# Chunk-selected attention into an ELU MLP on one core: w_in loaded in two pieces of eight chunks, both issued ahead of a fill

## The chip, the cores and the metric

The kernel runs on one core of a Trainium2 chip. The metric is the device time of one execution in microseconds (us). Each kernel was run several times; the median of the runs stands for it. One further execution was taken by the hardware profiler, and all views of the trace come from that one.

## The reference

The inputs are q, k and v of 4 batches, 8 heads, 768 positions and 64 dimensions, and two weight matrices, w_in (512 x 2048) and w_out (2048 x 512), all float32. For each head the keys are cut into chunks of 32. Each query gets an upper bound of its score with every chunk from the chunk's smallest and largest key in each dimension, takes the six best causal chunks, and attends to those alone:

```
ub     = sum(max(q * k_min, q * k_max), axis=-1)        # causal chunks only
sel    = the six chunks with the largest ub
attn   = softmax(where(sel & causal, q k^T / sqrt(64), -1e9)) @ v
x      = attn with the heads side by side               # 3072 tokens x 512
h      = x @ w_in
out    = where(h > 0, h, exp(min(h, 0)) - 1) @ w_out
```

## The kernel before

**Units of work.** The 3072 tokens are worked on in eight units of 384 (i = 0 to 7). Units 0 and 1 take the first half of batches 0 and 1 together, 192 positions of each at a time; the other six take one half of one batch each. For each unit the kernel loads k, q and v, transposes k and q on PE (operations kT and qT; L402 for the paired units, L543 for the others), computes the bounds (ub, L592) and the chosen chunks on DVE, the scores, their exponentials on ACT, and the product with v. Unit 0 covers only the first six chunks, so it needs no choice. The attention output is transposed into four tiles xt of 128 x 384.

**The MLP of a unit** (`mlp`, L844). For each of 16 column chunks fc of w_in, four matmuls on PE (h{i}.{fc}, L851) multiply a 128 x 128 block of w_in with the xt tiles into one PSUM bank; ACT takes the exponential (e, L858), POOL or DVE subtracts one (m, L860), and DVE combines them to the activated chunk (g, L864), which frees the bank. Then w_out is multiplied in (o{i}.{tt}.{c}, L875), and the result is copied out and stored.

**The weights.** w_in and w_out stay in SBUF in bfloat16. They are float32 in HBM, and the DMAs that load them are issued by POOL, which casts on the way. w_in comes in three pieces of columns: `load_w_in(0, 0, 4)`, `load_w_in(1, 4, 8)` and `load_w_in(2, 8, 16)` (L290 and L934). An operation h{i}.{fc} waits for the one piece with its chunk. w_out comes in four pieces (L296). All other loads, k, q, v (L304) and the copies of a constant into the score operand (econst, L304), are issued by SP, but for two at the start from ACT. They read rows of 64 float32.

**What sets the order.** The program is not scheduled by a tool. Each operation is added to a graph (`g.op`), with what it reads and writes; the string ORDER then lists all operations as triples of an engine letter (P, A, D, G for POOL, S for SP) and two digits in base 64 for the number of the operation in the graph (L944). Each engine takes its own operations in that order, one after the other, and waits where an operand isn't ready. PLACES gives the buffer slot of each new buffer in the order of its first use: slots of 11 load buffers f, 8 PSUM banks and so on.

**The stretch of the change.** In the order of the program, POOL's operations from v0p1 on are:

- v0p1: cast of a v load into the tile vext (L333), for the positions of unit 0
- rz: fill of the mask rows of rhs0 with zeros (L247), read from unit 2 on
- w_in1: DMA of chunks 4 to 7
- v0p0 and v1p0: two more casts of v
- w_in0: DMA of chunks 0 to 3
- ka10p0, a copy of keys, and ks1p1, a subtraction for the bounds
- w_in2: DMA of chunks 8 to 15
- tris2 (a triangular mask), more copies and fills, then the four DMAs of w_out among the MLP's m operations

PE's operations around the first MLP are, in its order: the products with v of unit 0, kT0s0, more products and the transposes into xt, kT0s1, h0.4, h0.6, h0.5, qT0s0, h0.3, qT0s1, h0.2, h0.1, h0.7, ub00, h0.0, h0.15, h0.9, h0.14, h0.12, h0.10, h0.8, a score matmul, h0.11, another, h0.13, and from there scores of unit 1 between the products with w_out. kT0s0 and kT0s1 read the two k loads of unit 1, batch 0; qT0s0 and qT0s1 read its two q loads. SP issues these four loads right behind the v loads of unit 0, and after them the k and q loads of unit 1, batch 1, and two copies of econst.

The f buffers of the casts v0p0 and v1p0 are handed to later loads by PLACES.

Of the kernel before, what the change touches and what calls it, by code (L numbers as in the profile page):

```python
# [42 lines left out]
P1DP26P25P1ED10G0-S2PS2vS2OD27D28D1FA1wP1YP20P2aGmDA0SP29D2bP1XA2cP1+D21G0JP1IP1OP1RP1SP1HS2IP2o  # L43
P1ND1GD1JD1ZD1KP2dG1dGmFA1-P1LD2qD1PA1QD2jD22P23D1TD1UD2eA2sD24A1MS2QP1VD1WG08G2uG0hP2BD2DD2CA2t
Pm-Pn6G2EAn7GbsGmGPn2Gn8D2pG2rAm+Dn0D14D0GAn3Dn4P2wPmWA2xA2yS2RP2JA2KDn5D2zPmSPmODn9Dn1AmXAmTD2L
GmYPnaGmHDmZAmPP3lAnbGmIA2FDmQDmUPmKAmLDmVD3nD3mA2MD3pGncPnGG2HPniA2AG07GmMA1fPnCG2SAnjD3oPnuD3q
D3rPnmDmRDmNG3tPneAnHA3sGnkDndAnvGnIP3HDnlAnDPnqGnwA3IDnJP41PnyDnxAnrA3uGnEDnFP3JP3+AnfPnQDnsS2k
A3KDntD2NAnnS3fG3LP2XA42P38PnRS2mA40GmJAnzA2GDnoD2ZDnpD2YP4lGngPnKPnXA4mD3vDnhA2+A30D43D3cP4DA4E
P4FG3ePnYA4GGnAD3aA3dD39D2-D31P4jD4HP3gG3bP33PnSS32S4+A34D35PnLA3hA4kD3iG3kS2TDnBP3wD4nS2VG2lG36
D3xG3jS50PnZPn-A2nD3yD3zA37S4-D3APnMPnTD3BD3CS4YD3GA3EG3FP3NDnUP4OP4MS4XS4ZP3MD3DP48P45A4PA4NP44  # L50
G2UG2WP4aD3ODn+D3PP4IP4JA4bP3SPnNA49D46D47A3TD4cS7UP3QD4QAnOP4sP4uP4dA3RP4eP4oS7SA4tP4pD4fP5rG3U
D4gA4vP4RD4KD4LP4SP4hA5sP5QS7WD4TD4UP3VP3WA5RD4qP5fP4VD3XD3YA5gS7RP5ED4rG4wP4xA4WP4yD5SP3ZA5FD4z
# [12 lines left out]
AppGpqDprDd1ApxGpyDpzAbrD8NPpUApVDpWPpYPqgApZGqeD8PA88Gp-Dp+Pq4Pq0Pq8PqkPqlPqwPqxD8QSc+Gd0AblAaK
Aq5Aq1Aq9DpXGq2Dq3Dq6Dq7DqfA8RP8VP9aPqmGqaDqbAd4AqhGqiDqjSbqSaLGaMA8WP9bA8IA9cD9dP97A98P8XA8YPqy
P8ZA8-P93A94P95A96P8+A90PqzP91A92D8TD8UDaXD8SP9kP9oPamP9yD8xGaZA9lA9zSaFPbzP9wAbADqAPqnA9xAanD99
P9fP9eP9sP9uP9BP9mSfrScTGd7ScVSfnSd3ScWDqoA9pA9vP9CA9DGhKD9AD9gD9hA9nA9tP9XA9YPqqD9EPa-P9iD9jP9q
A9rP9PPbEA9QP9FPaoAapP9RPa0P9GPa1A9SP9ZPqrP9VGaqAa2A9-Db7GbCDbFDb6SbnSpcSb8D9HD9IDbHDa+PagP9LP9T
ParP9NA9WA9UDb0D9+PqsPacPaePasDa3A9OPa5A9MPa4Dg2Dd8Db9DbaAahAafAatAadPaiPakAalAajPaaAabPdpPbuAbv  # L70
PbJGauPawPavP9JDa6Da7Pa8PqtGfoAbGAbKA9KAhIAb1Aa9DbcDbbDaxDayAfsAquDbBDbdDbeDbLPazDaAPdaGbfDdbGde
GddShDSd6DhESfpDbyDb2DfqSftPqGAqHGqIPqKPbgShxAqLDqMAbhAbwPraArbAbiAbjGrcAbIDqJDqNSbtSd9SfhSqvDrd
DfuGbNPreArfAbkAhQGrgDrhPrmArnPqWAqXAbxPriPbODbPGqYDqZDbQArjAhJPrqAdcGroDrpDbRGrkDrlGg8DbSPr2PqO
PqCGbMArrAbDGrsDrtAr3Gr4AqPGqQAdqAqDPqSAqTGqUAg1DbTDr5DbUDqRPdfAdgPryArzPdkAdlPq-Aq+GqEDqFDfvDqV
GbVGrAPr6PruAbXAr7DbYGr0Dr1DfxPrCPb+AdhArvAbWPbZAb-Ac0PrIGr8Dr9DrBPcdPrJPcbPc2PchAceAg5GrwGdiGc1
DrxDfwDdrAccPc3Ac4PcvPcgAciPcuPcFAcwGcjPcIPcJPcrAcsPrKPcpPcDPrLDc5DcfPc6Pc7AcKDcLSqBSfjShySfyDfz
# [904 lines left out]
```

## Time and profile before

| | |
|---|---|
| median of 3 runs | 281.04 us (280.64 to 281.32) |
| profiled execution | 281.25 us |
| its span, first to last instruction | 279.5 us |
| mean granted TensorE clock | 0.999 |
| DVE, ACT, POOL busy | 78%, 78%, 45% |
| DMA moved | 38.47 MB, mean 138 GB/s |
| queue q1 (issued by SP) | 98864 packets, 33.53 MB |
| queue q0 (issued by POOL: w_in, w_out) | 3696 packets, 4.19 MB |

A row of a timeline has its start, its length, the engine, the source line, the operation with the tiles it writes and reads, how many instructions of the kind were merged, and in brackets the idle time of the engine before it with what ended it. A row of the chain of waits has start, length and what ran. A row of a DMA issue has the tiles, the issuing queue, the number of DMAs, the size and the time from issue to landing. A row of a queue has its packets, its megabytes and the time that its packets took as a share of 16 DMA engines; where it is taken for a window, it counts that window alone. In the windows' rows each engine has its busy time and, in parentheses, its instructions; behind them stand the clock, the DMA share and GB/s.

### The profile page before, as it was taken

To read this page: it belongs to the slowest core of one execution; us is meant where nothing else is said; L and a number is where in the kernel's file an instruction comes from. 1 tells how busy PE (TensorE), PEld (TensorE's weight loads), DVE (VectorE), ACT (ScalarE), POOL (GpSimd) and SP (SyncE) were. 2 spreads that over 40 slices of the span, in tenths; PEclk is the share of its full clock that TensorE was granted. 3 is DMA by queue.
4 is the path that set the end of the run, shared out by engine and by line. 5 is a ranking of instruction groups with operands and counts; after the bars stand their busy time and mean duration, and the time that the engine had idled before them with its cause. 6 is when DMAs were issued, how large, how long until landed. Compare 5 with 4: busy or idle time off the path is not lost.

```text
span 279.5 us, 6918 instructions
## 1 busy us (share of the span) xinstructions
PE 263.2 (94%) x2436; PEld 162.9 (58%) x2436; DVE 217.4 (78%) x656; ACT 217.1 (78%) x493; POOL 125.5 (45%) x249
## 2 busy tenths in 40 slices
PE   1978899999999999999999999999999999999994
PEld 0745465785456755576555555666655556665553
DVE  4668978799978999979998999569797698424931
ACT  2596796789699998999999859886968579982620
POOL 8674745348521755422685736222541346310410
PEclk9999999999999999999999999999999999999999
DMA  8999999999529999946985499416600210042002
GB/s 163 198 211 211 199 211 210 217 202 251 123 60 203 247 219 230 196 115 112 171 203 114 109 226 206 84 36 136 170 4 0 60 39 1 16 139 82 15 17 96
DMA packets 103779, 38.47 MB, mean 138 GB/s; under 512 B 95168, under 2 KB 99520, under 8 KB 103744
## 3 DMA queue, kind: packets, MB, share of 16 engines
q1 hardware_dynamic: 98864, 33.53, 57.3%
q0 software_dynamic: 3696, 4.19, 8.7%
q10 hardware_dynamic: 1184, 0.30, 0.5%
q8 instruction: 19, 0.31, 0.5%
q14 instruction: 16, 0.13, 0.1%
HBM read 30.41 MB, written 6.29 MB: 131 GB/s over the span
## 4 chain that ended last, share of the span: by engine, by line
PE 70%; DVE 13%; DMA 8%; ACT 4%; issue 1%; POOL 1%; SPq 0%; DVEq 0%; ACTq 0%
PE bank L875 24%; PE bank L851 22%; PE bank L782 9%; DMA w_in_sb<-in_moe_w_in_dram 5%; PE bank L833 5%; DVE gT L864 2%; PE bank L592 2%; PE bank L402 2%; DMA kc<-in_k_dram 2%; ACT e L858 2%; DMA f<-in_k_dram 1%; PE bank L543 1%; PE bank L728 1%; PE bank L893 1%; DVE on L646 1%
## 5 line engine op out<-in xcount | busy, mean ns | idle before, releaser
L851 PE MATMUL bank<-xt,w_in_sb 128*128 128x384 bf16 x512 | 89.2, 326 | 2.2 <-DMA w_in_sb<-in_moe_w_in_dram 2.2
L875 PE MATMUL bank<-w_out_sb,gT 128*128 128x512 bf16 x368 | 89.5, 379 | 0.0
L860 POOL TENSOR_SCALAR m<-e 128x384 f32<-128x384 f32 x96 | 50.7, 536 | 59.3 <-ACT e L858 47.0
L864 DVE SCALAR_TENSOR_TENSOR gT<-bank,m 128x384 bf16<-128x384 f32 x128 | 65.9, 549 | 9.7 <-POOL m L860 8.4
L858 ACT ACTIVATE e<-bank 128x384 f32<-128x384 f32 x128 | 58.6, 493 | 16.7 <-PE bank L851 13.9
L851 PEld LDWEIGHTS <-w_in_sb 128*128 128x128 bf16 x512 | 49.1, 98 | 36.6 <-DMA w_in_sb<-in_moe_w_in_dram 3.0
L797 ACT ACTIVATE pt<-bank 128x384 bf16<-128x384 f32 (+1 forms) x144 | 67.0, 547 | 3.5 <-PE bank L782 2.1
L875 PEld LDWEIGHTS <-gT 128*128 128x128 bf16 x368 | 34.6, 97 | 35.7 <-issue 2.2
L782 PE MATMUL bank<-rhs,lhs 96*128 96x384 bf16 (+2 forms) x240 | 42.8, 293 | 1.0 <-DVE on L646 0.5
L814 POOL TENSOR_TENSOR pt<-pt,tri 128x256 bf16<-128x256 bf16 (+1 forms) x18 | 16.6, 924 | 39.3 <-ACT pt L801 20.1
L782 PEld LDWEIGHTS <-lhs 96*128 96x128 bf16 x240 | 21.7, 97 | 13.9 <-issue 0.9
L833 PEld LDWEIGHTS <-pt 128*128 128x128 bf16 x576 | 21.0, 97 | 4.0 <-DVE pt L814 0.4
L833 PE MATMUL bank<-vext,pt 128*128 128x65 bf16 x576 | 22.2, 193 | 0.3 <-DVE pt L814 0.3
L646 DVE TENSOR_TENSOR on<-bank,rcp 128x384 bf16<-128x384 f32 (+1 forms) x37 | 18.8, 509 | 1.2
L367 DVE TENSOR_REDUCE kst<-bank 128x12 f32<-128x384 f32 x32 | 16.6, 548 | 3.7 <-PE bank L402 2.8
L322 POOL CAST rhs<-qt 64x384 bf16<-64x384 f32 x23 | 12.3, 542 | 13.1 <-ACT qt L320 12.1
L636 DVE RECIPROCAL rcp<-bank 128x6 f32<-128x6 f32 (+1 forms) x40 | 7.3, 185 | 14.0 <-PE bank L833 8.7
L320 ACT ACTIVATE o<-bank 128x512 f32<-128x512 f32 (+1 forms) x13 | 7.5, 587 | 13.0 <-PE bank L875 10.1
L322 DVE COPY o<-bank 128x512 f32<-128x512 f32 (+1 forms) x12 | 7.9, 663 | 12.0 <-PE bank L875 10.0
L860 DVE TENSOR_SCALAR m<-e 128x384 f32<-128x384 f32 x32 | 13.1, 417 | 2.8 <-ACT e L858 2.6
L402 PE MATMUL bank<-ident_f,f 96*128 96x96 f32 x64 | 9.3, 295 | 6.2 <-DMA f<-in_k_dram 6.2
L814 DVE TENSOR_TENSOR pt<-pt,tri 128x512 bf16<-128x512 bf16 (+1 forms) x30 | 10.8, 376 | 5.3 <-ACT pt L801 3.5
(102 smaller groups left out, 338.6 us busy)
## 6 DMA issues: line engine op xcount, KB each, us to landing
f<-in_v_dram SPq DMA_DIRECT2D x22, 256.0 KB, 4.8
out_dram<-o SPq DMA_DIRECT2D x21, 256.0 KB, 3.4
f<-in_q_dram SPq DMA_DIRECT2D x18, 256.0 KB, 4.9
f<-in_k_dram SPq DMA_DIRECT2D x18, 256.0 KB, 4.7
kc<-in_k_dram SPq DMA_DIRECT2D x8, 384.0 KB, 4.3
w_out_sb<-in_moe_w_out_dram POOLq DMA_DIRECT2D x4, 512.0 KB, 10.5
f<-in_q_dram SPq DMA_DIRECT2D x6, 192.0 KB, 5.0
w_in_sb<-in_moe_w_in_dram POOLq DMA_DIRECT2D x2, 512.0 KB, 8.8
```

Source lines behind the costliest of these rows:

```text
L322: eng[e].tensor_copy(out=dst, in_=src)
L367: g.op(("kmin", "kmax")[w] + tag, (DVE,), lambda e, w=w, op=op: nc.vector.tensor_reduce(out=cs(w), in_=src(), axis=AX.X, op=op), reads=[(b ...
L646: nc.vector.tensor_tensor(out=ap(on)[:, 0:nt].rearrange("p q h d -> p h q d"), in0=view()[:, :, :, 0:D], in1=ap(rcp)[:, :, 0:nt].to_broadc ...
L782: nc.tensor.matmul(ap(banks[hd])[:, o + pc:o + pc + wd], lhsT=apl(ls, G)[0:96, pr, hd, P * kb:P * (kb + 1)], rhs=ap(rs)[0:96, hd, c0 - HS ...
L797: lambda e, hd=hd, pt=pt, banks=banks, wtot=wtot: nc.scalar.activation(out=ap(pt)[:, hd, PAD:PAD + wtot], in_=ap(banks[hd])[:, 0:wtot], fu ...
L814: eng[e].tensor_tensor(out=view, in0=view, in1=tri[:, 64:64 + P].rearrange("p (a b w) -> p a b w", a=1, b=1) .to_broadcast([P, 2, len(dg), ...
L833: nc.tensor.matmul(view()[:, hd, qi, :], lhsT=ap(pt)[:, hd, P * qi + off:P * qi + off + P], rhs=ap(vx[b])[:, kb, 2 * r + hd, :], start=(kb ...
L851: nc.tensor.matmul(ap(bank)[:, 0:HS], lhsT=w_in_sb[:, kk, P * fc:P * (fc + 1)], rhs=ap(xT[i, kk]), start=(kk == 0), stop=(kk == NKK - 1))
L858: g.op(f"e{i}.{fc}", (ACT,), lambda e, eb=eb, bank=bank: nc.scalar.activation(out=ap(eb), in_=ap(bank)[:, 0:HS], func=AF.Exp), reads=[(ban ...
L860: g.op(f"m{i}.{fc}", (POOL, DVE), lambda e, eb=eb, mb=mb: eng[e].tensor_scalar(out=ap(mb), in0=ap(eb), scalar1=-1.0, scalar2=1.0, op0=AOT. ...
L864: nc.vector.scalar_tensor_tensor(out=ap(gt), in0=ap(bank)[:, 0:HS], scalar=0.0, in1=ap(mb), op0=AOT.max, op1=AOT.min),
L875: nc.tensor.matmul(ap(bank), lhsT=ap(gts[fc])[:, P * tt:P * (tt + 1)], rhs=w_out_sb[:, fc, :], start=(fc == 0), stop=(fc == NFC - 1))
```

## The change

w_in is loaded in two pieces of eight chunks, 0 to 7 and 8 to 15. In POOL's order both stand ahead of the fill rz, with the casts v0p0 and v1p0 between them:

```
v0p1, w_in0 (0-7), v0p0, v1p0, w_in1 (8-15), rz, ka10p0, ks1p1, tris2, ...
```

The orders of PE, ACT, DVE and SP, operation by operation, are the same. Since there is one operation fewer in the graph, the numbers behind it in ORDER fall by one, and many rows of the string change in text alone. The casts v0p0 and v1p0 stand earlier in the program, so the load buffers f pass on in another rotation in PLACES; no other class of buffer changes. The core of the diff (of ORDER the one row that holds most of the stretch):

```diff
-S0+D0UP1qP1uD1cP18A1nD13S2gS2fG0CA1rP1hD19A1sG0nP1zD12S2hS2iP1yA1iP1AA1gA1mGmED0PA1CP1vA1xA1BG0A
+S0+D0UP1qP1uD1cP18A1nD13S2gS2fG0CGmDG0AG0-GmEG0nA1rP1hD19A1sP1zD12S2hS2iP1yA1iP1AA1gA1mD0PA1CP1v
...
-    for i, (c0, c1) in enumerate(((0, 4), (4, 8), (8, 16))):
+    for i, (c0, c1) in enumerate(((0, 8), (8, 16))):
         load_w_in(i, c0, c1)
```

In the row, G0C is v0p1, G0n is rz, G0A and G0- are v0p0 and v1p0, and GmD, GmE (and GmF further on, before the change) are w_in0, w_in1 (and w_in2).

More of the change, by code (lines that the diff above doesn't have):

```diff
@@ L47 @@
[L47 to L52, printed above, removed]
@@ new lines @@
+A1xA1BP1DP26P25P1ED10S2PS2vS2OD27D28D1FA1wP1YP20P2aA0SP29D2bP1XA2cP1+D21G0JP1IP1OP1RP1SP1HS2IP2o
+P1ND1GD1JD1ZD1KP2dG1dA1-P1LD2qD1PA1QD2jD22P23D1TD1UD2eA2sD24A1MS2QP1VD1WG08G2uG0hP2BD2DD2CA2tPmZ
+Pn5G2EAn6GbsGmFPn1Gn7D2pG2rAm-Dm+D14D0GAn2Dn3P2wPmVA2xA2yS2RP2JA2KDn4D2zPmRPmNDn8Dn0AmWAmSD2LGmX
+Pn9GmGDmYAmOP3lAnaGmHA2FDmPDmTPmJAmKDmUD3nD3mA2MD3pGnbPnFG2HPnhA2AG07GmLA1fPnBG2SAniD3oPntD3qD3r
+PnlDmQDmMG3tPndAnGA3sGnjDncAnuGnHP3HDnkAnCPnpGnvA3IDnIP41PnxDnwAnqA3uGnDDnEP3JP3+AnePnPDnrS2kA3K
+DnsD2NAnmS3fG3LP2XA42P38PnQS2mA40GmIAnyA2GDnnD2ZDnoD2YP4lGnfPnJPnWA4mD3vDngA2+A30D43D3cP4DA4EP4F
@@ new lines @@
+G3ePnXA4GGnzD3aA3dD39D2-D31P4jD4HP3gG3bP33PnRS32S4+A34D35PnKA3hA4kD3iG3kS2TDnAP3wD4nS2VG2lG36D3x
+G3jS50PnYPnZA2nD3yD3zA37S4-D3APnLPnSD3BD3CS4YD3GA3EG3FP3NDnTP4OP4MS4XS4ZP3MD3DP48P45A4PA4NP44G2U
+G2WP4aD3ODn-D3PP4IP4JA4bP3SPnMA49D46D47A3TD4cS7UP3QD4QAnNP4sP4uP4dA3RP4eP4oS7SA4tP4pD4fP5rG3UD4g
+A4vP4RD4KD4LP4SP4hA5sP5QS7WD4TD4UP3VP3WA5RD4qP5fP4VD3XD3YA5gS7RP5ED4rG4wP4xA4WP4yD5SP3ZA5FD4zP58
+D4AA5iS57P5kD5aA4iP4BA4CG7VS53P5JD3-P5xD59G5TG5uA5cS55D5BA5oA5NPokPoID5mA5GD5KPo4S5wAoJD5zS8lPow
+D5yGoKAo5SaND5LA5IPo8A5tDoLSn+G5bPocGo6AolD5lS51AoxG5MPogDo7G5nAo9SnOGomPoQA5OScZGoaDonAodPoED7T
@@ new lines @@
+A5hGoeAoRPooDobG5AA5jGoyDofPo0AoFGoSSnUDozAopPoAGoGDoTS7NAohGoqA5DPosDoHS7OAo1GoiDorP5VAotGo2Doj
+A5HGouDo3A5UG5PDovA5vPoMAoBG5dD5XPp0A52G7XD5WAoND5ZGoCPp1A5qGoOA5eD5YPpdPpeD5-SnVPp6D5+SaHPp7DoD
+A60G61DoPPpfD63A56DaOP66P6gA67P64DaQP6cP6iA65Pp2D62A6dDaPA6jP6mP68A6hP6lD5pP6aDaRP6eA6nPp8A69D54
+SaSG6oA6fP6BP6xD6kPoUA6bS7MA6CP6vA6yS7YP6qA6wP6HS7PP6pAoVP6zA6IS7QPoYD6rGoWD6sA6AG5CP6JDoXAoZP6t
+ScRP6MGbmP6ND6uA6KP7bGo-P7cP76A6OP6-Do+PpgA77D6LA7dD6PShFScXG7eDaTP6FA6+Pp3AphA6GP6DA6EP72P70P78
+P6RDp4A71A79DaUP6QDaVA73P7CP74A75P6YA6ZP7xP7zA7yA7ADaWP7ZD7aD6SSb3P6WA6XPp9ApaP7DSpiSp5G7BP8gA8h
@@ new lines @@
+D7-D81D6TD7+P7rP7lP7fP7gP7tP89P7pD8iA7EG7FD7hD7iD8aD8bG8kG8jP7vP8yD8zA7mA7sA7qA7uP7nA7oA7wP8mP6U
+P8FP7GScSSaCDb4A8CD8DG8EA6VA8dG8fP7HD7ID7JA8qP7jA7kP84A85P8tA8uAaIA8vD8oP7KD7LPpjPpDPpPPprPpLD8A
+D8rD8eG8cG80G82SaBSaGApEApQDb5D8BDaYD8nD8GGpFDpGAcYGpRDpSDboG8pG8sA86A8HDd5ApMDpNDpOPpHPpzApkGpl
+DpmApsP8KD8MD8LScUSaDSaESpcSaJShHApIApAA8JAbpG87GptG8wD8ODpuGpJDpKA83Ac-Gd2GpBDpCPqbAqcPpvPpnApo
+GppDpqDd1ApwGpxDpyAbrD8NPpTApUDpVPpXPqfApYGqdD8PA88GpZDp-Pq3Pp+Pq7PqjPqkPqvPqwD8QSc+Gd0AblAaKAq4
+Aq0Aq8DpWGq1Dq2Dq5Dq6DqeA8RP8VP9aPqlGq9DqaAd4AqgGqhDqiSbqSaLGaMA8WP9bA8IA9cD9dP97A98P8XA8YPqxP8Z
@@ new lines @@
+A8-P93A94P95A96P8+A90PqyP91A92D8TD8UDaXD8SP9kP9oPamP9yD8xGaZA9lA9zSaFPbzP9wAbADqzPqmA9xAanD99P9f
+P9eP9sP9uP9BP9mSfrScTGd7ScVSfnSd3ScWDqnA9pA9vP9CA9DGhKD9AD9gD9hA9nA9tP9XA9YPqpD9EPa-P9iD9jP9qA9r
+P9PPbEA9QP9FPaoAapP9RPa0P9GPa1A9SP9ZPqqP9VGaqAa2A9-Db7GbCDbFDb6SbnSpbSb8D9HD9IDbHDa+PagP9LP9TPar
+P9NA9WA9UDb0D9+PqrPacPaePasDa3A9OPa5A9MPa4Dg2Dd8Db9DbaAahAafAatAadPaiPakAalAajPaaAabPdpPbuAbvPbJ
+GauPawPavP9JDa6Da7Pa8PqsGfoAbGAbKA9KAhIAb1Aa9DbcDbbDaxDayAfsAqtDbBDbdDbeDbLPazDaAPdaGbfDdbGdeGdd
+ShDSd6DhESfpDbyDb2DfqSftPqFAqGGqHPqJPbgShxAqKDqLAbhAbwPr9AraAbiAbjGrbAbIDqIDqMSbtSd9SfhSquDrcDfu
@@ new lines @@
+GbNPrdAreAbkAhQGrfDrgPrlArmPqVAqWAbxPrhPbODbPGqXDqYDbQAriAhJPrpAdcGrnDroDbRGrjDrkGg8DbSPr1PqNPqB
+GbMArqAbDGrrDrsAr2Gr3AqOGqPAdqAqCPqRAqSGqTAg1DbTDr4DbUDqQPdfAdgPrxAryPdkAdlPqZAq-GqDDqEDfvDqUGbV
+GrzPr5PrtAbXAr6DbYGq+Dr0DfxPrBPb+AdhAruAbWPbZAb-Ac0PrHGr7Dr8DrAPcdPrIPcbPc2PchAceAg5GrvGdiGc1Drw
+DfwDdrAccPc3Ac4PcvPcgAciPcuPcFAcwGcjPcIPcJPcrAcsPrJPcpPcDPrKDc5DcfPc6Pc7AcKDcLSqASfjShySfyDfzSg3
+PclPrNPckPrCAcqGctDc8Dc9ShzSqoScaAcEAcGGcHDcxDcmDcnScoPcyPczDcADcBPrDScCGhPDfAPcMPcNDcODcPScQAdo
+AdjAdmPduPrEAg7ArLAdtAdsAdnGhGGhNGhMArFDfCPrOPrPPrQArRSfQShASrSSfiSrGPsjAskDdvDdwDdyDdxDdzDfEDdA
@@ new lines @@
+PsnAsoDspGslDsmDsqPrTArUGrVDrWShLPs3Ps7As8GdCPr+PrXPsHPebAs4Gs5Ds9DsaAs0Ds1DfBAdBPe5PsrDs2ArYGrZ
+Ae6AecDs6PsPAsIDsJDsKAssPdFPsbAdGPdLAsQAdMShOShBShCSfmSflGg4Sg6SfkPszPsvGstDfRDr-GsRAscGsdDsuPdN
+DsSAsAGsBAdOPdTPsfPsZDseAswDsxDsyAsgGshAdUPefAegDsiPedAeePsLDsCPdRPdXPe3PdHAsMDsNDsOPdWAdYAdSDdV
+PehPdPAdQPs-PdJGdDPeHAdIPsTPe9PeFAdKAe4AeiGdZPelPekPd+Pd-De0De1DdEAeaAeIAemGenPsDPs+AeGPeLDejPeK
+PezPe7PsUPeXAsEPepAe8PeoPevGsFDsGDfDAeYAeAAeMPeDAeEPeZPexPsVAewAe-DfFPeBAeCPetPsWPfGAeuDeqDerDfS
+AeyPf3PeVPeTDeJGeNDsXSsYDfUAf4Pf5Af6PeOPf8PePDeQPf9Pf1Pt3AeWAfaAeUSe2SfLSesPe+Af0DeRDf7Pt0Af2Dfb
@@ new lines @@
+PfcSeSPfdPhSPgkPgfPgpDfTAfHDt1DfeDfIDffSfgShRAhTGhVDfMDfNAglGgnAggAgoAgmAgqAgjPt4Pt5PgaPt6At7Agb
+GgeDfODfVDghDfPSt8St2SrMPtBAtCGtDDtEPttAgcAtuGtvAgsDtwPt9PtNAtaDtbDtcDfWPtpAfJAtqPtJGtrPu1AtKAgt
+GtLGfXDtsDtMAu2Gu3Du4AtOPtFPtdAtGGtHAgrAfKAteDtPDtQPfYAf+PtRPtxAtyAgiPthGtfGtzDfZAf-DtgDtIPtlAtm
+DtADg0PtVAtiGgdAhWPtZAtSDtnPguGtjAt-Pu5DtoDtkPufPugPu9DgwDtTDgyAtWAu6Gu7DtUPuaPubDgvDgxGt+GtXDgz
+DgAAgBAhUGgEDgDDu8DtYSg9PgLPgKAgMGgNPh7PhbPhaAhcPhpPgHPhoAhqAgIDu0PucPgFAgGPh5Ah8Ah6PhjPuhDgCPgT
+PgYDgJAhkDhrPgVPhlAgUAhmPgPPgOPuiDhdDh9PhfDgQDgRSgSAgWDhnPheDhgPgZDhhShiPi0PhXPhtPhsPi5Ag-Gg+Aud
```

82 lines of the change are left out of this document (20 added, 62 removed).

## The prediction

> **What bounds the kernel now.** I read the page first, then the chain of work that ended last up to 60 us, then the PE timeline around the one place where that chain leaves the engines.
>
> ```profile
> span 279.5 us, 6918 instructions
> PE 263.2 (94%) x2436; PEld 162.9 (58%) x2436; DVE 217.4 (78%) x656; ACT 217.1 (78%) x493; POOL 125.5 (45%) x249
> ```
> ```profile
> 6.56 0.74 PE bank L402 x3
> ...
> 10.29 0.85 PE bank L684 x2
> ...
> 18.06 13.64 DMA w_in_sb<-in_moe_w_in_dram
> ...
> 31.75 4.07 PE bank L851 x24
> ...
> 47.32 3.56 PE bank L875 x16
> ```
>
> TensorE is busy for 94% of the span. The chain (start, length, what) runs on PE, and at 18.06 it is a DMA: the third piece of w_in, issued then and waited for until 31.75. From there PE goes on without idle time (busy times by window, PE first):
>
> ```profile
> 32.00:57.00 25.00, 25.00 (x272) 16.49 (x271) 20.78 (x66) 18.79 (x40) 12.05 (x22) 1.00 1.16 212
> ```
>
> So what moves the start at 31.75 moves all that follows. The PE timeline shows what stands ahead of it:
>
> ```profile
> 22.40 2.12 PE L851 MATMUL bank<-xt,w_in_sb 128*128 128x384 bf16 x12
> 24.36 0.49 PE L402 MATMUL bank<-ident_f,f 96*128 96x96 f32 x4
> 25.89 0.82 PE L851 MATMUL bank<-xt,w_in_sb 128*128 128x384 bf16 x4 [1.04 <-DMA w_in_sb<-in_moe_w_in_dram]
> 26.55 0.49 PE L402 MATMUL bank<-ident_f,f 96*128 96x96 f32 x4
> 26.88 2.12 PE L851 MATMUL bank<-xt,w_in_sb 128*128 128x384 bf16 x12
> ...
> 29.74 0.82 PE L851 MATMUL bank<-xt,w_in_sb 128*128 128x384 bf16 x4
> 31.75 0.50 PE L851 MATMUL bank<-xt,w_in_sb 128*128 128x384 bf16 x2 [1.19 <-DMA w_in_sb<-in_moe_w_in_dram]
> ```
>
> The rows are h0.4, 6, 5 (22.40), the transposes qT0s0 (24.36), h0.3 after 1.04 us of waiting for the piece with chunks 0 to 3, qT0s1, h0.2, 1, 7, the bounds ub00, h0.0, and h0.15 after 1.19 us of waiting for chunks 8 to 15. PE takes its rows in this order, so the work from qT0s0 to h0.15 is 31.75 - 24.36 - 1.04 - 1.19 = 5.16 us.
>
> **The change on POOL.** Its timeline:
>
> ```profile
> 12.13 0.61 POOL L333 TENSOR_SCALAR vext<-f 64x512 bf16<-64x512 f32 x1
> 12.80 1.37 POOL L247 MEMSET rhs<- 32x1536 bf16 x1
> 14.12 0.98 POOL L291 DMA_DIRECT2D w_in_sb<-in_moe_w_in_dram  x1
> 15.18 1.35 POOL L333 TENSOR_SCALAR vext<-f 128x512 bf16<-128x512 f32 x2
> 16.48 0.80 POOL L291 DMA_DIRECT2D w_in_sb<-in_moe_w_in_dram  x1
> 17.33 0.49 POOL L322 COPY lhs<-kt 64x384 bf16<-64x384 bf16 x1
> 18.06 0.79 POOL L291 DMA_DIRECT2D w_in_sb<-in_moe_w_in_dram  x1
> ```
>
> Between 12.80 and 17.33 the same kinds stand before and after, one fill (1.37), two issues (0.98 and 0.80) and two casts (1.35), only in another order; the 1024 KB issue costs the 0.79 of a 512 KB one. So the copy at 17.33 stays, and the third issue (0.79) goes, in front of a tri select whose readers are the masks of the next attention stage, far behind: nothing. The casts end about 1.3 earlier than now: nothing either, a late cast could only have held PE up. The first issue moves from 14.12 to 12.80, 1.32 us earlier. The f buffers only change places. What decides is the DMA engines.
>
> **The two queues.** One row per DMA below, the landing counted from the issue: the pieces of w_in of 14.12, 16.48 and 18.06, then the q loads of 12.31 and 13.24 that qT0s0 reads.
>
> ```profile
> w_in_sb<-in_moe_w_in_dram POOLq DMA_DIRECT2D x1, 512.0 KB, 8.2
> ...
> w_in_sb<-in_moe_w_in_dram POOLq DMA_DIRECT2D x1, 512.0 KB, 9.4
> ...
> w_in_sb<-in_moe_w_in_dram POOLq DMA_DIRECT2D x1, 1024.0 KB, 13.6
> ...
> f<-in_q_dram SPq DMA_DIRECT2D x1, 192.0 KB, 5.0
> ...
> f<-in_q_dram SPq DMA_DIRECT2D x1, 192.0 KB, 5.1
> ```
>
> Pieces land at 22.3, 25.9 and 31.7, the q loads at 17.3 and 18.3. The next rows are packets by queue (q0 is POOL's, q1 SP's), from windows in this order: 16.5:16.7, 15.4:17.4, 17.4:17.6, 21.1:22, 22.5:24, 25.5:30.1, 20:21.
>
> ```profile
> q1 hardware_dynamic: 160, 0.04, 138.7%
> ...
> q1 hardware_dynamic: 1337, 0.33, 110.5%
> ...
> q0 software_dynamic: 40, 0.04, 122.5%
> ...
> q1 hardware_dynamic: 336, 0.09, 56.9%
> ...
> q0 software_dynamic: 224, 0.23, 89.6%
> q1 hardware_dynamic: 225, 0.07, 31.5%
> ...
> q0 software_dynamic: 407, 0.83, 95.2%
> q1 hardware_dynamic: 405, 0.11, 17.5%
> ...
> q1 hardware_dynamic: 769, 0.24, 99.3%
> q0 software_dynamic: 35, 0.03, 16.1%
> ```
>
> Alone, q1 moves 800 packets a us. Once q0 has work the two take turns packet by packet: 224 to 225 beside 1 KB packets, 407 to 405 beside the 2 KB packets of an eight-chunk piece, where each moves only 88 a us (405 in 4.6 us). The first piece starts on the engines 2.6 us after its issue (16.5:16.7 has no q0 row, the issue was at 14.12), and by 17.4 q1 has run dry: the q loads just get through in front of it. That is the margin which the change takes away.
>
> [...]
>
> **The sum.** The first piece, now 2 KB packets, starts at 12.80 + 2.6 = 15.4. Of the q loads 1337 packets are left then (those that q1 moved from 15.4 until it ran dry). In the first 0.9 us of sharing q1 gets 336 (window 21.1:22, a start of the same kind). The other 1001 go at 88 a us: 11.4 us, to 27.7. The two pieces have about 2 x 528 packets and last as long, if the second, issued at about 15.2, follows the first without a pause. From the last packet to the landing the second q load took 18.3 - 17.4 = 0.9. So it lands at **28.6** and not at 18.3. qT0s0 starts at 28.6 in place of 24.36; the 5.16 us of work follow, without the two waits, since the second piece lands with the q loads; h0.15 starts at 28.6 + 5.16 = 33.76, against 31.75: **2.0 us later**. Until then PE sits idle for 3 to 4 us behind h0.5. ACT and DVE lose as much (the copies of qT0s0 stand in their order), and behind 31.75 PE has no idle time to give back. The first piece lands at about 22.5 to 23.4, up to 1.0 after h0.4's 22.40: hidden by the longer stall.
>
> The k loads ahead of the q loads on q1 are through by 15.4, since 1337 is less than the 2 x 768 packets of the q loads alone (192 KB in rows of 64 float32): nothing. Loads behind the q loads fall back by several us, but their readers stand behind h0.15's group on PE, after 31.75 + 4.07 = 35.8, and q0 drains earlier in exchange: nothing, with up to 0.5 either way. Bounds of the q landing: 27.4 (a larger start share) to 29.6 (the slowest engine trails by 1 us), so +0.8 to +3.0.
>
> The profiled execution took 281.25 us, 1.75 outside the span, and 0.2 above the median 281.04 of the three runs. 281.25 + 2.0 = 283.25; less 0.2, **283.0**, own range 281.8 to 284.0.
>
> **Rivals.** *A pause between the pieces (faster, 0.30).* The second piece of before was issued at 16.48, yet 20:21 shows q0 with 35 packets and q1 with 769: q0 ran dry between the first two pieces. If that belongs to a drained ring and not to the 4.6 us since the issue, it comes again at about 21.6 (16.3 + (528 - 65)/88), and the 530 q packets then left pass in 0.7 us: the q loads land at about 23, in time. It decides at a pause of 0.7 us. For: the same two issues, 2.4 us apart. Against: 4.6 us after the new second issue is 19.8, before the first piece is drained. Then both waits go (2.23), h0.4 is 0.5 late, and h0.15 comes 1.7 earlier; but DVE holds it back:
>
> ```profile
> 33.17 2.38 DVE L864 SCALAR_TENSOR_TENSOR gT<-bank,m 128x384 bf16<-128x384 f32 x5
> 35.82 1.03 DVE L864 SCALAR_TENSOR_TENSOR gT<-bank,m 128x384 bf16<-128x384 f32 x2 [0.28 <-POOL m L860]
> ```
>
> DVE has no gap up to 35.5, and the banks of h0.8 and h0.11 come free with the first and third of the five of 33.17, at about 33.7 and 34.6, whatever the DMA does. I take 0.9 of the 1.7: 280.1.
>
> *A short pause (0.12).* Half the q packets slip through, qT0s0 starts at 25.5 to 27, the stall about equals the waits removed: 280.6 to 281.6, say 281.1.
>
> *The stall also costs PE its speed (slower, 0.08).* Two matmuls of 512 columns take 0.85 in the chain at 10.29, sixteen take 3.56 at 47.32: 0.425 against 0.22 each, PE having started at 6.56 after idling. So PE runs slow after idle time, for some 5 us. If the stall does that, the 5.16 us of work behind it cost about 2.4 more: 285.4. PE's longest idle stretch behind the start is now 1.19, so no row shows how much it takes. [...]
>
> *The change does not do what it says:* excluded, the order of POOL is fixed by the string, and its issues wait for nothing.
>
> **Numbers.** Forecast 0.50 (283.0), pause 0.30 (280.1), short pause 0.12 (281.1), slow PE 0.08 (285.4). 0.2% is 0.56 us, about what a measurement of this kernel tells from no change. Faster: 0.30 + 0.02 of the short pause = 0.32; same: 0.10; slower: 0.50 + 0.08 = 0.58. The range 279.7 to 284.2 takes in the pause and the bounds of the q landing, and leaves out the slow PE and the ends.
>
> **What would show it.** Right: a PE wait of 3 to 4 us in front of L402 at 24.4 to 25.2, ended by a DMA into f from in_q; the q load of 13.24 landing at 27.4 to 29.6; no window between 16 and 27 in which q0 is empty; no wait for w_in at h0.3 or h0.15; h0.15 at 32.5 to 34.7. Wrong: qT0s0 at about 24.5 to 25.4 and q1 with several hundred packets in a stretch near 21.6 (the pause), or q1 far above q0 in packets while both work (turns by more than a packet).

## The result and the profile after

The changed kernel takes 282.74 us (median of 8 runs, 282.28 to 284.91), the kernel before 281.28 us (8 runs, 280.64 to 281.42): a ratio of 1.0073, 95% interval 1.0044 to 1.0102. It is slower by 1.46 us. The profiled execution of the changed kernel took 282.98 us, 1.73 more than that of before (281.25).

The page of the changed kernel, span and busy times:

```profile
span 281.2 us, 6915 instructions
...
PE 264.7 (94%) x2436; PEld 163.4 (58%) x2436; DVE 216.6 (77%) x656; ACT 217.5 (77%) x493; POOL 125.1 (44%) x248
```

The span grew by 1.7 us. The chain of waits (start, length, what) says through what:

```profile
13.26 15.37 DMA f<-in_q_dram
...
28.67 0.47 PE bank L402 x3
...
32.89 4.66 PE bank L851 x28
...
49.04 3.56 PE bank L875 x16
```

The piece of w_in that stood in the chain of before, 18.06 to 31.70, is gone. In its place stands a load of q, issued at 13.26 and landed at 28.63; the row at 28.67 is the rest of qT0s0, which reads it. The row at 32.89 begins with h0.0. In PE's timeline below, h0.0 starts at 32.82 with four matmuls of 0.16 us each, so h0.15 starts at 33.48 in place of 31.75, 1.73 later. From there on the distance stays: the block of w_out that was at 47.32 is at 49.04, 1.72 later, and the span ends 1.7 later. So all of the loss arises ahead of 33.5.

PE's timeline of the changed kernel, from the last transposes on:

```profile
22.08 0.50 PE L402 MATMUL bank<-ident_f,f 96*128 96x96 f32 x4
23.61 3.63 PE L851 MATMUL bank<-xt,w_in_sb 128*128 128x384 bf16 x12 [1.03 <-DMA w_in_sb<-in_moe_w_in_dram]
27.08 0.25 PE L402 MATMUL bank<-ident_f,f 96*128 96x96 f32 x1
28.67 0.47 PE L402 MATMUL bank<-ident_f,f 96*128 96x96 f32 x3 [1.35 <-DMA f<-in_q_dram]
28.98 0.81 PE L851 MATMUL bank<-xt,w_in_sb 128*128 128x384 bf16 x4
29.63 0.50 PE L402 MATMUL bank<-ident_f,f 96*128 96x96 f32 x4
29.96 2.12 PE L851 MATMUL bank<-xt,w_in_sb 128*128 128x384 bf16 x12
...
32.82 4.72 PE L851 MATMUL bank<-xt,w_in_sb 128*128 128x384 bf16 x28
```

Two things are new. PE waits for the q load at 28.67. And h0.4, 6 and 5, the row at 23.61, take 3.63 us, where the same twelve matmuls took 2.12 before. The busy times by window, for 19.9:23.3, 23.3:26.7 and 26.7:30, have the reason in their column for the granted clock, the third number from the end:

```profile
19.90:23.30 3.40, 1.74 (x16) 0.89 (x14) 3.18 (x12) 2.92 (x11) 1.07 (x2) 1.00 1.13 207
23.30:26.70 3.40, 3.09 (x10) 1.49 (x11) 0.87 (x2) 0.32 (x1) 1.35 (x4) 0.50 1.13 205
26.70:30.00 3.30, 1.95 (x16) 1.35 (x15) 1.73 (x7) 1.84 (x5) 0.79 (x2) 1.00 1.24 237
```

For 3.4 us PE ran at half its clock, after a window in which it had been busy for 1.74 of 3.4 us. By these rows that costs nothing in this execution: at full clock the row would have ended 1.5 us earlier, and PE would have waited for the q load for 2.9 us instead of 1.35.

The rows of the two pieces and of that q load (size, time from issue to landing; issues at 12.90, 15.32 and 13.26), then the packets of the two queues in 16:18, 16:27 and 21:27:

```profile
w_in_sb<-in_moe_w_in_dram POOLq DMA_DIRECT2D x1, 1024.0 KB, 10.7
...
w_in_sb<-in_moe_w_in_dram POOLq DMA_DIRECT2D x1, 1024.0 KB, 14.1
...
f<-in_q_dram SPq DMA_DIRECT2D x1, 192.0 KB, 15.4
...
q0 software_dynamic: 185, 0.38, 101.3%
q1 hardware_dynamic: 218, 0.05, 17.5%
...
q0 software_dynamic: 999, 2.01, 96.5%
q1 hardware_dynamic: 995, 0.25, 16.8%
...
q0 software_dynamic: 550, 1.09, 95.8%
q1 hardware_dynamic: 550, 0.14, 17.6%
```

The two pieces follow each other without a pause: over 11 us q0 (w_in) and q1 (all that SP loads) have as many packets each, 999 and 995, in six of these exactly 550 each. q1 moves a quarter of a MB in the time in which q0 moves two.

### The profile page after: what moved, and what is told of

It is laid out like the page before. It is cut to its first block, busy times and chain, and to the rows that moved or that the text cites. A ratio compares the mean times of both kernels' runs of the same rounds, so it can differ in the third digit from the quotient of the medians.

```text
span 281.2 us, 6915 instructions
## 1 busy us (share of the span) xinstructions
PE 264.7 (94%) x2436; PEld 163.4 (58%) x2436; DVE 216.6 (77%) x656; ACT 217.5 (77%) x493; POOL 125.1 (44%) x248
## 4 chain that ended last, share of the span: by engine, by line
PE 71%; DVE 14%; DMA 7%; ACT 3%; issue 1%; POOL 1%; SPq 0%; DVEq 0%; ACTq 0%
PE bank L875 24%; PE bank L851 23%; PE bank L782 9%; DMA f<-in_q_dram 5%; PE bank L833 5%; PE bank L592 2%; DVE gT L864 2%; PE bank L402 2%; DVE kst L367 2%; DVE on L646 2%; ACT e L858 2%; DMA f<-in_k_dram 2%; PE bank L543 1%; PE bank L728 1%; DVE kn L493 1%; PE bank L893 1%
## 5 line engine op out<-in xcount | busy, mean ns | idle before, releaser
L851 PE MATMUL bank<-xt,w_in_sb 128*128 128x384 bf16 x512 | 90.7, 330 | 1.0 <-DMA w_in_sb<-in_moe_w_in_dram 1.0
L851 PEld LDWEIGHTS <-w_in_sb 128*128 128x128 bf16 x512 | 49.7, 99 | 36.2 <-issue 4.3
L782 PEld LDWEIGHTS <-lhs 96*128 96x128 bf16 x240 | 21.7, 97 | 13.9 <-issue 1.0
L860 DVE TENSOR_SCALAR m<-e 128x384 f32<-128x384 f32 x32 | 12.5, 396 | 4.4 <-ACT e L858 4.1
```

Of the source, the lines that this page charges most:

```text
L782: nc.tensor.matmul(ap(banks[hd])[:, o + pc:o + pc + wd], lhsT=apl(ls, G)[0:96, pr, hd, P * kb:P * (kb + 1)], rhs=ap(rs)[0:96, hd, c0 - HS ...
L851: nc.tensor.matmul(ap(bank)[:, 0:HS], lhsT=w_in_sb[:, kk, P * fc:P * (fc + 1)], rhs=ap(xT[i, kk]), start=(kk == 0), stop=(kk == NKK - 1))
L860: g.op(f"m{i}.{fc}", (POOL, DVE), lambda e, eb=eb, mb=mb: eng[e].tensor_scalar(out=ap(mb), in0=ap(eb), scalar1=-1.0, scalar2=1.0, op0=AOT. ...
```

## The experiments

**The theory** after these rows: the early first piece reaches the DMA engines ahead of the last q load, the second follows without a pause, the q load gets one packet for each packet of 2 KB and lands at 28.6, and PE, with other work ready, waits for it. **The rivals:** the pieces of eight chunks cost by themselves, through the first one's later landing; and the half clock costs. "In time" below means that PE does not wait for the load. Each experiment was timed in the same session as the kernel before, whose medians were 281.34, 281.23 and 281.13 in the three sessions; a difference between kernels of two sessions is uncertain by about as much as these differ. POOL's order is written with the names of the operations; each edit in ORDER moves or adds just these triples, and PLACES changes where the first use of a buffer moves with them.

### The two pieces, but behind the fill

```diff
-v0p1, w_in0 (0-7), v0p0, v1p0, w_in1 (8-15), rz, ka10p0
+v0p1, rz, w_in0 (0-7), v0p0, v1p0, w_in1 (8-15), ka10p0
```

> The changed kernel with one thing undone: its two pieces of eight chunks stay, but the fill rz goes back ahead of both of them, so that they are issued at about 14.3 and 16.5 in place of 12.9 and 15.3. Theory (what costs is that the first piece starts on the DMA engines while the q loads still have 1337 packets to move; 1.4 us later almost all of these are through): the q load of 13.26 lands at 18 to 19.5 in place of 28.6, PE does not wait for it, the first piece lands at about 23, h0.15 starts at about 30.4, and the time is about 280.4 (279.8 to 281.2), below both kernels. Rival (it is the pieces of eight chunks themselves, with packets of 2 KB and one landing for eight chunks, that cost): the time stays at 282 or above.

Measured: 282.99 us (12 runs, 281.54 to 284.18), ratio 1.0048 (1.0029 to 1.0068). The q load was in time (landed at 17.7), as the theory has it, and the gain it promised did not come. PE's timeline, and its window from 20 to 31:

```profile
20.87 0.84 PE L402 MATMUL bank<-ident_f,f 96*128 96x96 f32 x4
24.98 4.02 PE L851 MATMUL bank<-xt,w_in_sb 128*128 128x384 bf16 x12 [3.26 <-DMA w_in_sb<-in_moe_w_in_dram]
28.79 0.84 PE L402 MATMUL bank<-ident_f,f 96*128 96x96 f32 x4
```
```profile
20.00:31.00 11.00, 7.55 (x34) 4.43 (x35) 4.84 (x15) 3.94 (x11) 3.20 (x7) 0.53 1.14 206
```

The first piece landed at 24.9 (on 15 of 16 DMA engines by 23.2), and h0.4 waited 3.26 us for it; I had expected about 23. And the clock was at one half for some 10 us, well into the work behind the wait. So the time sits on the rival's side, but with two causes mixed: the landing of the piece and the clock. The experiments with fills below separate them.

### The three pieces of before, early

```diff
-v0p1, rz, w_in1 (4-7), v0p0, v1p0, w_in0 (0-3), ka10p0, ks1p1, w_in2 (8-15)
+v0p1, w_in1 (4-7), v0p0, v1p0, w_in0 (0-3), rz, ka10p0, ks1p1, w_in2 (8-15)
```

> The kernel before with its three pieces (4, 4 and 8 chunks), but with the fill rz behind the second one, so that the first two are issued at about 12.9 and 15.3, as in the changed kernel. Theory (turns of one packet each; beside packets of 1 KB the q loads move 150 a us, not 88, and there are only half as many bytes in front of them): the first piece starts at about 16, the q load of 13.26 lands at 20 to 23, in time for qT0s0 at about 24.4, and the time is 280.0 to 281.3. Rival (any issue of w_in ahead of the fill makes the q loads late, whatever the size of the piece): q load at 26 or later and the time at 282.3 or above.

Measured: 280.19 us (9 runs, 279.47 to 280.51), ratio 0.9959 (0.9942 to 0.9975): faster than both kernels. Issuing early is not what costs; it gains. PE's timeline, where no wait of a microsecond is left:

```profile
22.38 2.17 PE L851 MATMUL bank<-xt,w_in_sb 128*128 128x384 bf16 x12
24.38 0.50 PE L402 MATMUL bank<-ident_f,f 96*128 96x96 f32 x4
24.71 0.81 PE L851 MATMUL bank<-xt,w_in_sb 128*128 128x384 bf16 x4
...
30.09 3.42 PE L851 MATMUL bank<-xt,w_in_sb 128*128 128x384 bf16 x20 [0.18 <-DMA w_in_sb<-in_moe_w_in_dram]
33.82 0.81 PE L851 MATMUL bank<-xt,w_in_sb 128*128 128x384 bf16 x4 [0.30 <-DVE gT L864]
```

h0.15 starts at 30.09, 1.66 earlier than before, and then a bank of DVE's is waited for, as the first rival of the prediction had it; 1.15 us remain of it. The time came as expected, but not by the mechanism that I had written down. The packets of the queues in 16:18 and 18:20:

```profile
q0 software_dynamic: 389, 0.40, 121.7%
q1 hardware_dynamic: 20, 0.00, 1.5%
...
q1 hardware_dynamic: 1002, 0.25, 63.3%
q0 software_dynamic: 213, 0.20, 60.0%
```

No even shares in the first two microseconds, 389 to 20; and then a pause of q0 in which q1 moves most of 1002 packets, so that the last q load lands at 21.7. The piece of four chunks (512 KB in packets of 1 KB) is through before the next, issued at 14.84, starts between 19 and 20: by 19 q0 had sent 516 packets, and a piece has 528. A piece of eight is not: in the changed kernel q0 had sent 282 packets by 19 and 524 by 21.7.

### The second piece behind tris2

```diff
-v0p1, w_in0, v0p0, v1p0, w_in1, rz, ka10p0, ks1p1, tris2
+v0p1, w_in0, v0p0, v1p0, rz, ka10p0, ks1p1, tris2, w_in1
```

> The changed kernel with its second piece (chunks 8 to 15) issued behind tris2, at about 18.7 in place of 15.3; the first piece stays early. Theory (the q loads are late because the second piece follows the first without a pause; a piece starts on the engines up to 4.6 us after its issue, so a pause of about 1 us opens near 22): the q load lands at about 23 to 24.5, qT0s0 starts by 25, the second piece lands at about 30 to 31, and the time is about 280.6 (280.1 to 281.5). Rival (the second piece follows the first at once even so, because its descriptors are ready long before): q load at 27.5 to 28.6 and 282.7 as in the changed kernel.

Measured: 282.65 us (11 runs, 280.71 to 285.24), ratio 1.0054 (1.0025 to 1.0082). Undecided: the second piece was issued at 17.54, the q load had landed on 15 of 16 DMA engines by 23.3, and on the last one at 28.16; PE waited for that one. A load in time on 15 engines gained nothing here.

### Two chunks ahead of qT0s0

```diff
-PE: h0.4, h0.6, h0.5, qT0s0, h0.3, qT0s1, h0.2, h0.1
+PE: h0.4, h0.6, h0.5, h0.3, h0.2, qT0s0, qT0s1, h0.1
```

ACT's exponentials of the two chunks and DVE's products of h0.6 and h0.4 move with them, ahead of the copies of q.

> The changed kernel with its DMAs as they are, and with h0.3 and h0.2 ahead of qT0s0 in PE's order (and their exponentials and the products of h0.6 and h0.4 ahead of the copies of q on ACT and DVE). Theory (what makes the changed kernel late is PE waiting for the q load, with other work ready): the two chunks, 1.3 to 1.6 us of PE work, fill the wait of 1.35, h0.15 starts 1.1 to 1.3 earlier, and the time is about 281.5 (281.1 to 281.9). Rival (the q load is late, but the time is set by something else that the change moved, such as the first piece of w_in or the buffers of the loads): 282.4 or above.

Measured: 282.23 us (12 runs, 281.71 to 283.31), ratio 1.0033 (1.0017 to 1.005): 0.5 below the changed kernel, between the two expectations. In its profile the clock was at one half from 22.1 to 28.9, so that the two chunks took 1.3 us each and filled the wait without leaving a gain.

### The second piece at 22

```diff
-v0p1, w_in0, v0p0, v1p0, w_in1, rz, ka10p0, ks1p1, tris2, ka10s0, kq
+v0p1, w_in0, v0p0, v1p0, rz, ka10p0, ks1p1, tris2, ka10s0, w_in1, kq
```

> The changed kernel with its second piece issued far later, behind the copy of keys that waits for ACT until 22.2, so at about 22.7; the first piece of eight chunks stays early. In the run with the second piece behind tris2, 15 of 16 DMA engines had landed the q load of 13.12 by 23.3 and the last one at 28.16, so there the pause was missing on one engine. Theory (the late q load is the cause): with a pause on all engines the q load lands at 22.5 to 24, PE does not wait for it; the second piece lands at about 31 to 32, and h0.15 starts then: 280.5 to 281.6, near the kernel before. Rival (the first piece of eight chunks, in time for h0.4 only at about 22.8 to 23.6, and the clock that falls in the thin work before it, cost as much without the q load): 282.3 or above.

Measured: 282.24 us (12 runs, 280.89 to 283.04), ratio 1.0028 (1.0011 to 1.0046). Here the q load was in time on all engines (23.61), and no wait for it is left; yet the median fell by only 0.5. The executions tell why: the three with a mean clock of 0.992 to 0.994 took 280.89 to 281.11, the nine at 0.988 took 281.88 to 283.04. 3.4 us of half clock more (3.4 of 281 us at one half is 0.006 of the mean) cost 1 to 2 us here. Nothing is waited for behind it that could hide it; the same kernel with fills, below, comes to 281.18.

### The changed kernel with fills

40 matmuls on zeros, whose result nobody reads, keep PE busy where it waited.

```diff
+PE: 3 fills ahead of each of pxp0, pxp2, pxp1 and kT0s1, 8 ahead of h0.4, 20 ahead of qT0s0
```

> The changed kernel with 40 matmuls on zeros added to PE's order, whose results are not used: 3 ahead of each of the last three transposes into xt and of kT0s1, 8 ahead of h0.4 and 20 ahead of qT0s0, where PE waited. In the changed kernel's profile the granted clock fell to 0.5 from 23.30 to 26.71, in front of the wait for the q load. Theory (thin work of PE in about 19 to 23 lets the clock fall; in the profiled execution the wait for the q load hides it; its two executions of 284.7 and 284.9 are ones in which it falls on work behind the wait): a clock of 0.997 or above in every execution, h0.15 at 33.5 as before, a median of 282.5 (282.1 to 283.0), and no execution above 283.6. Rival (the slow clock itself is what the changed kernel pays): median at 281.6 or below. Second rival (the clock has nothing to do with PE's work): clocks from 0.98 to 0.994 as before.

Measured: 282.84 us (6 runs, 282.02 to 283.10), ratio 1.0056 (1.0035 to 1.0078). Every execution had a mean clock of 0.998 or above, against 0.982 to 0.994 in the changed kernel. With PE at work where it had waited, the clock stayed up, and the changed kernel's median does not depend on it: 282.84 with, 282.74 without fills. Its two executions at 284.74 and 284.91 have no match here (highest 283.10), which fits a half clock on work behind the wait; with 6 executions against 8 and no trace of the two, that is not shown.

### The late two pieces with fills

```diff
+PE, on top of "behind the fill": 3 fills ahead of each of pxp0, pxp2, pxp1 and kT0s1, 24 ahead of h0.4
```

> The kernel with two pieces issued behind the fill (first issue 14.1; q loads in time at 17.7; first piece landing at 23.2 on 15 engines and at 24.93 on one; granted clock 0.5 from 20.51 to 30.75), with 36 matmuls on zeros added in PE's order: 3 ahead of each of the last three transposes into xt and of kT0s1, 24 ahead of h0.4. Theory (of its median of 283.0, the part above 281.5 is the half clock): a clock of 0.997 or above, h0.4 at 23.3 to 25, the 5.16 us of work at full speed behind it, h0.15 at 30.5 to 32.3, and the time 280.4 to 281.8. Rival (the late landing of the first piece is the whole of it): 282.7 or above.

Measured: 281.51 us (12 runs, 280.86 to 282.71), ratio 1.0016 (1.0001 to 1.003), clock 0.997 to 1.0. So about 1.4 of that kernel's 282.99 was the half clock: 1.48 by the two medians, 1.37 with each taken against the kernel before of its own session. What remains is the first piece: it landed at 24.47, and h0.4 started at 24.98 (the fills, a little too many, ran until then) instead of 22.40. That is 2.58 late; the two waits of before, 2.23 together, are gone, and the work between is 0.33 shorter, so that h0.15 starts at 31.77, where it started before (31.75). The median is 0.28 above the 281.23 of before, and where that arises is not shown.

### The q loads one place later, w_in as before

```diff
-SP: ldk0s10, ldk0s00, ldq0s00, ldq0s10, ldk1s10, ec000
+SP: ldk0s10, ldk0s00, ldk1s10, ldq0s00, ldq0s10, ec000
```

> The kernel before, its three pieces of w_in as they are, with one edit on SP: the k load of unit 1, batch 1, that was issued at 14.48 goes ahead of the two q loads that qT0s0 reads. These are then issued about 1 us later, at the places where a k load landed at 20.6 to 22.8 and a copy of econst at 21.1 to 23.6, and behind the start of the first piece. Theory (a late q load costs its landing plus 5.16 us of work, less 31.75, once that is above 0): the second q load lands at 22 to 30 (its slowest engine decides); landing at t, the time is 281.3 + max(0, t + 5.16 - 31.75), so 281.3 for 26.6 or earlier, 283.3 for 28.6. Rival (PE's wait for q does not set the time): 281.3 whatever t is.

Measured: 281.14 us (12 runs, 280.55 to 281.86), ratio 1.0002 (0.9988 to 1.0015). It tells nothing apart: the second q load landed at 23.87, in time, and both sides then expect no change.

### The second piece at 22, with fills

```diff
+PE, on top of "the second piece at 22": 3 fills ahead of each of pxp0, pxp2, pxp1 and kT0s1, 8 ahead of h0.4
```

> The kernel with the second piece issued at about 22.1 (q load in time at 23.6, second piece landing at 31.2), with the 20 matmuls on zeros of the filled kernel ahead of the transposes into xt, of kT0s1 and of h0.4; the 20 ahead of qT0s0 are left out, since nothing is waited for there. Beside the changed kernel with fills (282.84) it has the same first piece, the same pieces of eight chunks and the same full clock; only the second piece is late instead of the q load. Theory (with the clock kept up, the late q load is what the changed kernel pays): q load at 22.5 to 24.5, no wait for it, h0.15 at 31 to 31.9 when the second piece lands, and 280.6 to 281.5. Rival (the first piece of eight chunks pays it): 282.3 or above.

Measured: 281.18 us (12 runs, 280.49 to 282.37), ratio 1.0003 (0.9985 to 1.0021). This and the changed kernel with fills (282.84) are the pair that decides: the same first piece at the same place, full clock in both, and the second piece issued at 15.15 in one and at 22.11 in the other, which leaves the q loads room. (Besides, the 20 fills ahead of qT0s0 stand in the filled kernel alone.) The packets in 21.6:22.6, and PE's timeline:

```profile
q1 hardware_dynamic: 988, 0.27, 115.8%
q0 software_dynamic: 11, 0.01, 7.8%
```
```profile
23.66 2.12 PE L851 MATMUL bank<-xt,w_in_sb 128*128 128x384 bf16 x12 [0.48 <-DMA w_in_sb<-in_moe_w_in_dram]
25.62 0.50 PE L402 MATMUL bank<-ident_f,f 96*128 96x96 f32 x4
...
31.20 4.07 PE L851 MATMUL bank<-xt,w_in_sb 128*128 128x384 bf16 x24 [0.57 <-DVE ubT L609]
```

In one microsecond almost without q0, q1 moves 988 packets, and the q load is there at 24.3. The row of 31.20 names an operation of DVE that ended at 31.14 as what PE waited for; the second piece landed at 31.15, so both ended that wait together. The pair differs by 282.84 - 281.18 = 1.66 us, or by 1.56 with each taken against the kernel before of its own session. Up to some 0.4 of that can be the 20 fills: in the profile of the filled kernel they ran 0.4 past the landing of its q load, which came early there, at 27.42. So the late q load is worth about 1.2 to 1.7 us; against the changed kernel without fills, 282.74, the difference is 1.56. That the first piece of eight chunks lands at 23.6 costs nothing against the kernel before, since that one waits 2.23 further on.

### Two chunks ahead of qT0s0, with fills

```diff
+PE, on top of "two chunks ahead": 3 fills ahead of each of pxp0, pxp2, pxp1 and kT0s1, 8 ahead of h0.4, 10 ahead of qT0s0
```

> The kernel with h0.3 and h0.2 ahead of qT0s0 and the DMAs of the changed kernel, with matmuls on zeros: 3 ahead of each of the last three transposes into xt and of kT0s1, 8 ahead of h0.4, 10 ahead of qT0s0. Without them it took 282.23, and its two chunks ran at a clock of 0.5 (1.3 us each). Theory (with the clock kept up, two chunks of 0.65 us fit into the wait for the q load and are no longer behind it): 1.3 below the changed kernel with fills, 281.5 (281.1 to 282.0), clock 0.997 or above. Rival (the end is not set by the q load and the work behind it): 282.4 or above.

Measured: 282.19 us (12 runs, 281.46 to 282.95), ratio 1.0038 (1.0023 to 1.0053), clock 0.998 or above. The direction is the theory's, half of the size: 0.65 below the changed kernel with fills, not 1.3. PE's timeline has the rest:

```profile
28.55 0.80 PE L402 MATMUL bank<-ident_f,f 96*128 96x96 f32 x7 [0.58 <-DMA f<-in_q_dram]
29.60 1.74 PE L851 MATMUL bank<-xt,w_in_sb 128*128 128x384 bf16 x8 [0.25 <-ACT qt L320]
```

With the chunks gone from between the transposes, h0.1 and h0.7 follow at once, and they write the banks that qT0s0 and qT0s1 have just filled; they wait for ACT to copy these out, 0.25 ahead of the first, and the second one within the row of 29.60, until ACT's copy ends at 30.5. From the landing of the q load, 28.51, to h0.15, 32.74, are still 4.2 us, where the changed kernel took 4.85 (28.63 to 33.48).

### The kernel before with a few fills

```diff
+PE, on top of the kernel before: 2 fills ahead of each of pxp0, pxp2, pxp1 and kT0s1
```

> A control: the kernel before with 2 matmuls on zeros ahead of each of the last three transposes into xt and of kT0s1, and nothing else. Theory (in the kernel before the waits for w_in at h0.3 and h0.15, 2.2 us together, hide a half clock in 22 to 26, so keeping it up gains nothing; eight matmuls of 0.11 us delay h0.4 by at most 0.4, which the same waits hide): 281.0 to 281.6. Rival (the kernel before pays for the clock too, so that a part of the difference between the two kernels is chance in the clock): 280.7 or below.

Measured: 281.13 us (12 runs, 280.75 to 283.14), beside 281.13 of the kernel before in the same session, ratio 1.0012 (0.9993 to 1.0031). The fills cost and gain nothing there, and the waits for w_in (0.68 and 1.15 in its profile) still stand ahead of h0.3 and h0.15. Among the 88 executions of the kernel before in the three sessions, the 31 with a mean clock of 0.996 or above have a median of 281.12, the 12 below 0.990 one of 281.48. So the clock is worth some 0.4 us there, and the difference of 1.46 between the two kernels is not chance in the clock.

## Why the prediction was right, step by step

The forecast was 283.0, measured are 282.74; the profiled execution was to take 283.25 and took 282.98. The mechanism is the one on record, and the pair of 282.84 and 281.18 shows it; that the landing of the q load came out to within 0.03 us is luck. By its steps:

- *POOL*: the copy that was to stay at 17.33 started at 17.58, 0.25 late, because the first cast waited 0.28 for its v load. Nothing hung on it.
- *Start of the first piece*: forecast 15.4; issued at 12.90 instead of 12.80, and its first packets show at 15.8 to 16.0, 2.9 after the issue instead of 2.6. That is 0.4 to 0.6 us more of q1 alone, at 800 packets a us (160 in 15.6:15.8) some 320 to 480 packets that the loads of SP gained.
- *The sharing*: 1:1 at about 90 packets a us held from 20 on (550 to 550 in six microseconds), and there was no pause, which was the doubtful point. But the start was harder on q1 than assumed: 218 packets in 16:18 and 143 beside 183 of q0 in 18:20, together 361, where 336 in 0.9 us and 88 a us after that would have made 609. The profile of before had a sign of it. The prediction read 17.4:17.6, with no packet of q1, as q1 having run dry; but the k load issued at 14.48 had still to come (it landed at 22.79), and in 17:18 q1 moved 83 packets beside 178 of q0. The start to go by was that one, of the first piece, and not the one at 21.1. The even counts, besides, do not show turns of one packet, as the prediction takes them: if both queues sent several packets per turn, counts over a microsecond would be even too. In ten windows of 0.1 us from 21 to 22, with 5 to 16 packets of each queue, the two counts are at most 4 apart; the turns of a single engine are not shown. The sum needs the even shares alone.
- *The q load*: forecast 28.6, landed 28.63. The first two errors leave 72 to 232 packets in the load's favour (320 to 480 less 248), which is 0.8 to 2.6 us at 90 a us; and on 15 of its 16 DMA engines the load had landed by 27.60, 1.0 before the forecast. The last engine came 1.03 later, and the forecast had such an engine in its upper bound alone. The errors cancelled, and the agreement is better than the working. In other kernels with the same DMA orders it landed at 27.42, 28.31 and 28.51, inside the bounds of 27.4 to 29.6.
- *PE's wait*: forecast one stretch of 3 to 4 us. Measured 1.03 for the first piece, 1.35 for the q load, and 1.5 lost to the half clock between. The sum was right, its form wrong: the first piece landed at 23.6, past the 23.4 of the estimate, and the clock fell before there was any long wait.
- *The work behind it*: 5.16 us forecast, 33.48 - 28.67 = 4.81 measured; one of the four transposes of qT0s0, whose load had landed early, ran ahead at 27.08.
- *h0.15*: 33.76 forecast, 33.48 measured, +1.73 in place of +2.0; and as said it goes through to the end undiminished (1.72 at w_out, 1.7 in the span). The experiments bear this step out: in the profiles of all thirteen kernels here the span ends 247.5 to 248.5 us after the start of h0.15, while that start itself lies anywhere from 30.09 (three pieces early) to 34.59 (two pieces behind the fill). So that start sets the time to within 1 us, whatever it waits for.
- *The waits for w_in* at h0.3 and h0.15 are gone, as forecast. *The first piece* was to be hidden by the longer stall: it is, in this kernel; in the kernel with late pieces it was what PE waited for, 3.26 us.

The rivals: the *pause between the pieces* did not come. The first piece starts 2.6 us after its issue in the kernel before and 2.9 in the changed kernel, the second of the three early pieces 4.2 to 5.2 after its own; in the changed kernel the second piece was issued at 15.32, and the first one kept the engines until about 22 (524 packets by 21.7), so no gap was left between them. Why a piece takes that long to start is not shown. But the rival's consequences were right where a pause does open: q1 moves the rest in about 1 us, and the kernel with three early pieces ends at 280.19, the rival had 280.1. *The stall costs PE its speed*: the slow clock did come, though in front of the stall and not behind it, and was hidden there. I had let it depend on the length of a single idle stretch; what length that takes, and with it the chance of 0.08, was my estimate, and no run shows it. In this trace 0.7 us of the wait from 22.58 on were all that lay ahead of the fall at 23.30, with PE busy for 1.74 of the last 3.4 us. The price named for it, about 2.4 us, was not paid in the median; two executions of the changed kernel are 2 us above it, and why stays open.

## What to carry to other kernels

A bulk DMA that goes out earlier can be slower for the kernel (282.74 against 281.28 us here): ask which small loads of another queue are still to come when its first packet reaches the engines, and count packets, not bytes: here the queue with packets of 256 B moved 550 of them in the six microseconds in which the one with packets of 2 KB moved 550. Splitting the bulk load so that its first part was through before the next one started gave the other queue its pause back here (most of 1002 packets in 18:20): the same early issue with pieces of four chunks gained 1.15 us where pieces of eight lost 1.46. And when an edit moves a wait, look at the granted clock ahead of it: a fill of idle PE made two of these comparisons readable that otherwise mixed two causes.

## What the runs showed of the hardware

**The clock fell on thin work.** The stretches of half clock lasted 3.4 us in the changed kernel (mean 0.50 in 23.3:26.7), 6.8 with the second piece at 22, and 10.2 with the late two pieces (20.5:30.7). The rows of the second, for 18.7:22.1, 22.1:25.5 and 25.5:28.9:

```profile
18.70:22.10 3.40, 2.15 (x20) 1.21 (x19) 3.04 (x13) 2.98 (x12) 0.50 (x2) 1.00 1.15 221
22.10:25.50 3.40, 2.46 (x8) 1.16 (x9) 1.44 (x3) 0.13 (x1) 2.74 (x5) 0.50 1.10 172
25.50:28.90 3.40, 3.40 (x14) 2.09 (x13) 1.82 (x7) 2.38 (x5) 0.79 (x2) 0.50 1.12 215
```

PE had been busy for 2.15 of 3.4 us, with no gap above 0.46 us, when the clock fell at about 22.1; and it stayed low (0.50) through a window in which PE waited for 1.09, and through the one after it. It was back only behind that window of full work (3.40 of 3.40 us). The start of the stretch lies elsewhere in each execution (23.3, 20.5, 22.1). No threshold is settled here: in the profile of the changed kernel a window with 2.34 of 3.4 us busy (16.5:19.9) left the clock up.

**The first packets of a POOL piece pushed q1 aside.** 389 packets of q0 to 20 of q1 in 16:18 in the kernel with three early pieces, where a later window has even counts (94 to 90 in 19.6:20.2); 102 to 0 in 17:18 in the changed kernel. No run here tells why.

**One DMA engine trailed.** The first piece landed on 15 of 16 engines at 23.2 and on the last at 24.9 in the kernel with late pieces; with the second piece behind tris2, one engine held the q load back by 4.9 us (23.3 to 28.16), and PE with it. In the changed kernel the last engine of the q load came 1.03 us behind the other 15 (27.60 and 28.63).
